# Stage one of the second batch without folds, its pairs spread wider, two weight parts loaded sooner

## The chip, the core and the metric

The kernel runs on one core of a Trainium2 chip. The metric is device time in microseconds (us) of that core. Engines are named PE (TensorE), DVE (VectorE), ACT (ScalarE), POOL (GpSimd) and SP (SyncE, which here only issues DMAs); PEld is the weight load of PE.

## The reference

Eight batches of 3008 x 256 tokens go through a Fourier layer (a real transform along the 3008 tokens, a complex 256 x 256 product with a bias, a soft threshold, the transform back), and all 24064 tokens then go through a two-layer network of width 2048 with a squared ReLU:

```python
X = np.fft.rfft(x, axis=1)
Yr = Xr @ w_r - Xi @ w_i + b_r
Yi = Xr @ w_i + Xi @ w_r + b_i
Yr = np.sign(Yr) * np.maximum(np.abs(Yr) - lam, 0.0)   # Yi likewise
y = np.fft.irfft(Yr + 1j * Yi, n=3008, axis=1)
...
h = y.reshape(24064, 256) @ w_in
g = np.maximum(h, 0.0) ** 2
out = g @ w_out
```

## The kernel before

The transform of 3008 = 64 x 47 points is done in products. **Stage one** (`Fwd`, 13 pieces q per batch) takes a piece of x of shape 120 x 2 x 256: row n2 and its mirror image lie side by side as parts 0 and 1. `add` folds them on POOL into sum and difference (tile xs), `run` multiplies the sum with the cosine matrix and the difference with the sine matrix (two fp32 products into one psf bank, line L237), ACT copies the bank to xe (one buffer), and SP stores xe to the DRAM tensor s1. **Stage two** works on pairs of frequency groups (`Pair`, 12 per batch): load ka from s1 and the matrix kb, `fwd` (L281), split into high and low fp32r parts (kxh, kxl), the 256 x 256 mix (L302), bias and threshold, and `back` (L334), whose result is stored to the DRAM tensor s3. **Stage three** (`Back`, L441 to L445) loads du from s3 and finishes the inverse transform of a piece, and `Tokens` makes of it the seven operands yt of a Strassen product on POOL (ms and yt). **The network**: six tiles of some 500 tokens per batch, eight steps (`Step`) per tile. A step has 21 products psh with w_in (L464), the recombination on DVE (mp, mu, mv, mc), ReLU, square and a cast on ACT, the low part mg on POOL, and 12 products pso with w_out.

Batch 0 has a way of its own, ahead of all that: a **ring** of seven double pieces (`Fwd32`, folds on DVE and POOL), then 24 **units** (`Unit32`) of stage two and back in plain fp32 (L381, L395, L406). Meanwhile the network's weights, which come as doubles in 16 parts (`moe_part`), are turned on DVE and ACT into fp32r pairs (`convert`: the six operations of `bits` and `join`, L151 to L164, and then `split` or `win_sums`). Parts 0 to 9 are converted beside the units, parts 10 and 11 before the network starts, and parts 12 to 15 in the network's half-steps 1, 3, 5 and 7.

From then on everything hangs on the loop over half-steps m (two per step, 96 per batch, called slots within a batch). Beside the network of batch b, a list of jobs, each with a slot at which it is due, runs stage two of batch b+1 and stage one of batch b+2. In the steady batches a pair is due every 6.1 slots and a piece of stage one every 7.0. Beside batch 0 more must be done: stage one of batch 1 (due from slot 10.2, every 1.2 slots), then its pairs (from slot 26.0, every 4.1), and stage one of batch 2 (from slot 21.6, every 5.4). Within a pair the next load is due 3.7 slots ahead of its `fwd`.

The order of instructions on each engine is fixed when the program is built, by a planner with a simulated time line; an engine then takes them strictly in that order. `issue_after` adds an edge of order on one engine. All loads of x, ka, kb and du go through `load_next`, which chains them on SP's queue in the order of the jobs:

```python
def load_next(out, in_, eng=nc.sync):
    with tc.issue_after(chain[eng].ins):
        chain[eng] = eng.dma_start(out, in_)
```

So a load that waits for its buffer holds back all loads behind it. Buffers: xt 2, xs 1, xe 1, ka 2, kb 1, du 1 in the loop. Tiles of the conversion (big, small, dw, ds) keep their memory until the last part is converted; only then is the memory of the list SIDE (xs, xt, xe and the tiles of stage two) opened.

Of the kernel before, what the change touches and what calls it, by code (L numbers as in the profile page):

```python
# [9 lines left out]
F32 = mybir.dt.float32  # L10
# [13 lines left out]
B, S, D, FF = 8, 3008, 256, 2048  # L24
# [3 lines left out]
R, J = 5, 13  # L28
M1 = R * G
# [3 lines left out]
LAM = 0.01  # L33
NP1 = N1 + 1
FRONT = {
    "a32": 1, "b32": 1, "w320": 1, "w321": 1, "big": 5, "small": 6, "ds": 1, "dw": 4, "ka": 5, "xe": 7,
    "kv": 3, "psf": 6,
}
MAIN = {
    "xs": 1, "xe": 1, "du": 1, "kv": 1, "kp": 1, "kq": 1, "ksh": 1, "ksl": 1, "kxl": 1, "kb": 1, "yr": 1,  # L40
    "ms": 1, "mp": 1, "mu": 1, "mv": 1, "mc": 3,
}
CONV = ("big", "small", "dw", "ds")
SIDE = ("xs", "xt", "xe", "ka", "kb", "kcm", "kxh", "kxl", "kp", "kq", "ke", "kv", "ksh", "ksl", "kuh", "kul", "ku")

# [11 lines left out]
def fnet_moe(ctx: ExitStack, tc, x, w_r, w_i, b_r, b_i, w_in, w_out, bm, cm, dx, a32, c32, out):  # L59
    nc = tc.nc  # L60
    pe, act, dve, pool = nc.tensor, nc.scalar, nc.vector, nc.gpsimd
# [7 lines left out]
    am32 = const.tile([M1, 2, M1], F32, name="am32")  # L69
    dx_sb = const.tile([128, 2, 4 * N2], F32R, name="dx_sb")  # L70
    bias = const.tile([128, 2, D], F32, name="bias")
# [16 lines left out]
    def T(name, shape, dt, tag=None):  # L88
        tag = tag or name
        return pools.get(tag, phase["pool"]).tile(shape, dt, name=name, tag=tag, bufs=phase["bufs"].get(tag, 2))  # L90

    def bank(shape, name="psf"):
        return phase["psum"].tile(shape, F32, name=name, tag=name, bufs=phase["bufs"].get(name, 1))

    def copy(eng, out, in_):
        if eng is act:
            return act.copy(out=out, in_=in_)  # L97
        return eng.tensor_copy(out=out, in_=in_)  # L98
# [5 lines left out]
    chain = {}  # L104
# [7 lines left out]
    b32 = T("b32", [128, D], F32)  # L112


    def load_mix_weights():
        for j, v in enumerate((b_r, b_i)):
            with tc.issue_after(ring[3].folds[1].ins):
                pool.dma_start(b32[64 * j:64 * j + 64, :], v.unsqueeze(0).broadcast_to([64, D]))
            with tc.issue_after(ring[-1].folds[1].ins):
                pool.dma_start(bias[:, j, :], v.unsqueeze(0).broadcast_to([128, D]))  # L120
        for j, w in enumerate((w_r, w_i)):
            st = T(f"w32{j}", [128, 2, D], F32)
            w32.append(st)
            nc.sync.dma_start(st, w.rearrange("(c p) d -> p c d", p=128))
        wd = T("wd", [128, 2, D], F32, tag="small")
        wn = T("wn", [128, 2, D], F32, tag="small")
        sub(dve, wd, w32[1], w32[0])
        dve.scalar_tensor_tensor(out=wn, in0=w32[0], scalar=-1.0, in1=w32[1], op0=ALU.mult, op1=ALU.subtract)
        for j, w in enumerate((wd, wn, w32[0])):
            copy(act, wx[0][:, j], w)  # L130
            sub(dve, wx[1][:, j], w, wx[0][:, j])
# [73 lines left out]
    class Fwd:  # L205
# [23 lines left out]
        def add(self):  # L229
            self.u = T("xs", [M1, 2, D], F32)  # L230
            for t in range(2):
                self.fold(pool, self.u[:, t:t + 1], t)

        def run(self):
            ps = bank([128, 2, D])
            for t in range(2):
                nc.tensor.matmul(ps[:M1, t], am32[:, t], self.u[:, t], start=True, stop=True)  # L237
            self.ev = T("xe", [M1, 1, 2, D], F32)
            copy(act, self.ev[:, 0], ps[:M1])
            self.store()  # L240
# [3 lines left out]
    def store_back(b, g, ps, eng):  # L244
        uh = T("kuh", [128, D], F32R)
        ul = T("kul", [128, D], F32R)
        done = copy(act, uh, ps)
        if eng is None:
            sub(dve, ul, ps, uh)
        else:  # L250
            u = T("ku", [128, D], F32)
            done = copy(act, u, ps)
            sub(eng, ul, u, uh)
        rows = s3[b].rearrange("m p c -> (m p) c")
        for v, m in ((uh, 4 * g), (ul, 128 + 4 * g if 4 * g < 64 else 32 + 4 * g)):
            nc.sync.dma_start(rows[m * NP:m * NP + 128], v.bitcast(F32))
        return done


    class Pair:  # L260
# [70 lines left out]
        def back(self, g):  # L331
            ps = bank([128, 512])
            for n, (j, r) in enumerate(((0, self.sh), (1, self.sh), (0, self.sl))):
                nc.tensor.matmul(  # L334
                    ps[:, :D], self.cm[:, g, j * 128:(j + 1) * 128], r[:, g], start=n == 0, stop=n == 2
                )
            store_back(self.b, self.g + g, ps[:, :D], None)

# [240 lines left out]
    def fwd_tasks(b, start, step):  # L581
        jobs = []
        for q in range(J):
            f, at = Fwd(b, q), start + q * step
            jobs += [(at - 2.5, f.load), (at - 0.8, f.add), (at + 0.3, f.run)]
        return jobs
# [17 lines left out]
    def at(items, n, *names):  # L604
        if 0 <= n < len(items):
            for name in names:
                getattr(items[n], name)()

    ring = [Fwd32(0, q, 2) for q in range((J + 1) // 2)]
    units = [Unit32(0, g) for g in range(G)]  # L610
    parts = [moe_part(q) for q in (0, 1, 8, 9, 2, 3, 10, 11, 4, 5, 12, 13, 6, 7, 14, 15)]
# [8 lines left out]
    with tc.issue_after(ring[2].last.ins):  # L620
        load_mix_weights()


    EARLY, LATE = 2, 6
    LATER = {1: 12, 3: 13, 5: 14, 7: 15}

    def convert(n, after=None):
        p = parts[n]
        p.bits(after)
        p.join()  # L630
        if n % 4 > 1:
            p.split()
        elif n % 4:
            win_sums(n // 4, parts[n - 1:n + 1])

    last = ring[-1].last
    for p in parts[:EARLY]:
        with tc.issue_after(last.ins):
            p.load()
        last = p.get  # L640
# [4 lines left out]
    for r in range(-5, len(units) + 3):  # L645
        at(units, r + 5, "load")
        at(units, r + 1, "fwd", "bins")
        at(units, r - 1, "shrink")
        at(units, r - 2, "back", "store")
        at(units, r, "mix")  # L650
        while loads and loads[0][0] <= r:
            p = loads.pop(0)[1]
            with tc.issue_after((units[r + 5] if r + 5 < len(units) else units[-1]).get.ins):
                p.load()
        for n, k in paced:
            if k + 3 == r:
                convert(n, units[k])
    with tc.issue_after(ring[-1].folds[1].ins):
        pool.dma_start(dx_sb, dx)
    chain[nc.sync], chain[pool] = units[-1].get, ring[-1].folds[1]  # L660
    front.close()
    phase.update(
        pool=memory(ctx, "main"), bufs={**{k: FRONT[k] for k in CONV}, **MAIN, "psf": 2}, psum=memory(ctx, "main_ps", space=PSUM)
    )

    pairs = [[Pair(b, j) for j in range(G // 2)] for b in range(B)]
    steps = [Step(t, n) for t in range(len(tiles)) for n in range(NF // 2)]
    slots = len(HALF) * NF
    first = sorted(back_tasks(0, 0), key=lambda j: j[0])
    for name in ("load", "mm", None):  # L670
        for _, job in first:
            if (job.__name__ if job.__name__ in ("load", "mm") else None) == name:
                job()
    for n in range(len(parts) - LATE, len(parts) - LATE + 2):
        convert(n, units[-1])
    jobs = []
    for m in range(2 * len(steps) + 4):
        b, r = divmod(m, slots)
        if r == 0 and b < B:
            jobs = [(t - slots, job) for t, job in jobs]  # L680
            if b + 1 < B:
                first, step = 1.0, 6.1
                if b == 0:
                    first, step = 26.0, 4.1
                    jobs += fwd_tasks(1, 10.2, 1.2) + [(first - 0.8, pairs[1][0].load)]
                jobs += pair_tasks(pairs[b + 1], first, step)
            if b + 2 < B:
                first, step = (2.6, 7.0) if b else (21.6, 5.4)
                jobs += fwd_tasks(b + 2, first, step) + [(95.0, pairs[b + 2][0].load)]
            for j in range(len(HALF)):  # L690
                t = b * len(HALF) + j + 1
                if t < len(tiles):
                    jobs += back_tasks(t, NF * j + 0.5)
            jobs.sort(key=lambda j: j[0])
        n, k = divmod(m, 2)
        if k and 0 <= n - 2 < len(steps):
            steps[n - 2].out(1)
        if n < len(steps):
            (steps[n].second if k else steps[n].first)()
        if not k and 0 <= n - 2 < len(steps):  # L700
            steps[n - 2].out(0)
        if m in LATER:
            convert(LATER[m], steps[n])
        if m == max(LATER):
            conv.close()
            pools.update(dict.fromkeys(CONV), **dict.fromkeys(SIDE, memory(ctx, "side")))
        while jobs and jobs[0][0] < r + 1:
            jobs.pop(0)[1]()
# [86 lines left out]
```

## Time and profile before

| what | us |
|---|---|
| median of 3 runs | 2666.55 |
| lowest, highest | 2664.07, 3630.81 |
| the profiled execution's own time | 2664.53 |
| its span, first to last instruction | 2662.8 |

The profile is of one execution. Its page gives busy times of the engines; its views give them by stretch of the span, with the TensorE clock that was granted (1.00 is full speed), or list groups of instructions, the chain of work that ended last, and the waits. A product in fp32 stands as two matmul records, one in fp32r as one.

### The profile page before, as it was taken

What the parts mean: (1) busy time and instruction counts of PE and PEld (TensorE: products, weight loads), DVE (VectorE), ACT (ScalarE), POOL (GpSimd) and SP (SyncE); (2) the same over time, 40 slices, a digit from 0 to 9 for tenths busy, and PEclk for the clock granted to TensorE, in tenths of its full rate; (3) what the DMA queues carried; (4) which work ended last, traced back from release to release, by engine and by line L of the source; (5) the groups of instructions that cost most, each with busy time, mean ns of one, the idle gap of its engine ahead of it and who ended that gap; (6) DMA issues with size and microseconds to landing.
All of it is one profiled execution on the core that took longest, in us unless ns stands there. A gap on an engine that the chain in (4) does not pass through costs nothing.

```text
span 2662.8 us, 47497 instructions
## 1 busy us (share of the span) xinstructions
PE 2578.3 (97%) x16856; PEld 2353.4 (88%) x16856; DVE 1786.7 (67%) x3797; ACT 1675.3 (63%) x2432; POOL 1678.3 (63%) x1656
## 2 busy tenths in 40 slices
PE   6788989999999999999999999999999999999999
PEld 4677978899999999999998999999999999999998
DVE  6873766576676767667676776757766667766554
ACT  3455655566666666666666666666666666666665
POOL 3266655567666666766676666766766666666564
PEclk8898989999999999999999999999999999999999
DMA  8614333333332333323333233323333222221100
GB/s 250 209 49 123 103 115 90 100 105 100 105 96 77 100 104 106 91 74 106 110 96 88 83 103 104 98 88 95 105 101 98 67 83 80 86 64 40 39 16 16
DMA packets 191262, 250.50 MB, mean 94 GB/s; under 512 B 21755, under 2 KB 135667, under 8 KB 191027
## 3 DMA queue, kind: packets, MB, share of 16 engines
q1 hardware_dynamic: 178627, 224.85, 27.2%
q0 software_dynamic: 12400, 22.61, 3.7%
q8 instruction: 135, 2.21, 0.3%
q14 instruction: 100, 0.82, 0.1%
HBM read 146.85 MB, written 100.53 MB: 93 GB/s over the span
## 4 chain that ended last, share of the span: by engine, by line
PE 90%; DVE 3%; DMA 3%; issue 1%; POOL 1%; ACT 1%; SPq 0%; POOLq 0%; ACTq 0%; DVEq 0%
PE pso L464 38%; PE psh L464 34%; PE psf L302 7%; PE psf L281 3%; PE psf L237 3%; PE psf L334 2%; PE psf L444 1%; PE psf L445 1%; PE psf L441 1%; PE psf L395 1%; POOL mg L101 1%; DMA kb<-bm_in 1%; DMA s<-xe 1%; DMA du<-s 0%; PE psf L353 0%
## 5 line engine op out<-in xcount | busy, mean ns | idle before, releaser
L101 POOL TENSOR_TENSOR mg<-mc,mg 128x500 fp32r<-128x500 f32 (+1 forms) x768 | 974.0, 1289 | 596.4 <-ACT mg L97 536.7
L464 PE MATMUL pso<-mg,wout 128*128 128x500 f32 (+1 forms) x4608 | 1179.6, 393 | 1.8 <-ACT mg L97 1.3
L464 PE MATMUL psh<-yt,win 128*128 128x250 f32 (+1 forms) x8064 | 1083.2, 282 | 14.1 <-DVE mc L464 8.2
L464 PEld LDWEIGHTS psh<-yt,win 128*128 128x128 f32 x8064 | 1029.0, 190 | 48.4 <-issue 8.9
L464 ACT ACTIVATE mc<-mc 128x1000 f32<-128x1000 f32 (+1 forms) x768 | 802.6, 1045 | 414.1 <-DVE mc L464 404.4
L464 PEld LDWEIGHTS pso<-mg,wout 128*128 128x128 f32 x4608 | 822.4, 189 | 134.2 <-POOL mg L101 3.3
L464 DVE TENSOR_TENSOR mc<-psh,mv 128x500 f32<-128x500 f32 (+3 forms) x768 | 419.3, 547 | 432.6 <-PE psh L464 400.1
L97 ACT CAST mg<-mc 128x1000 fp32r<-128x1000 f32 (+1 forms) x384 | 397.0, 1034 | 19.0 <-ACT mc L464 0.4
L464 DVE TENSOR_TENSOR mv<-psh,mu 128x500 f32<-128x500 f32 (+1 forms) x384 | 260.8, 679 | 56.1 <-PE psh L464 23.1
L302 PE MATMUL psf<-wx,kxh 128*128 128x256 f32 x1008 | 209.4, 284 | 3.9 <-ACT kxh L97 2.9
L98 DVE COPY mp<-psh 128x250 f32<-128x250 f32 (+1 forms) x384 | 159.9, 416 | 51.2 <-PE psh L464 28.6
L216 POOL TENSOR_TENSOR xs<-xt 120x256 f32<-120x256 f32 x182 | 133.2, 752 | 88.8 <-DMA xt<-x_in 82.9
L302 PEld LDWEIGHTS psf<-wx,kxh 128*128 128x128 f32 x1008 | 167.7, 190 | 8.6 <-ACT kxh L97 3.6
L101 POOL TENSOR_TENSOR ksl<-kv,ksh 128x512 fp32r<-128x512 f32 x84 | 108.6, 1293 | 105.4 <-ACT ksh L97 105.4
L464 DVE TENSOR_TENSOR mu<-psh,mp 128x250 f32<-128x250 f32 (+1 forms) x384 | 160.7, 419 | 11.7
L464 DVE TENSOR_TENSOR mc<-psh,mp 128x250 f32<-128x250 f32 (+1 forms) x384 | 157.1, 409 | 7.4 <-PE psh L464 5.6
L323 DVE TENSOR_TENSOR kv<-psf,ke 64x256 f32<-64x256 f32 x336 | 141.8, 422 | 21.7 <-PE psf L302 10.6
L302 PE MATMUL psf<-wx,kxl 128*128 128x256 f32 x504 | 142.1, 282 | 2.4 <-DVE kxl L101 2.4
L97 ACT COPY dy<-psf 128x188 f32<-128x188 f32 x256 | 76.5, 312 | 92.7 <-PE psf L445 92.4
L314 DVE TENSOR_TENSOR ke<-psf,bias 128x512 f32<-128x512 f32 x84 | 58.0, 691 | 106.5 <-PE psf L302 106.3
L97 ACT CAST kuh<-psf 128x256 fp32r<-128x256 f32 x192 | 68.2, 373 | 92.6 <-PE psf L334 71.9
L451 DVE TENSOR_TENSOR yr<-psf,dy 128x188 f32<-128x188 f32 (+4 forms) x256 | 78.0, 313 | 72.1 <-ACT dy L97 65.2
(94 smaller groups left out, 2538.3 us busy)
## 6 DMA issues: line engine op xcount, KB each, us to landing
du<-s SPq DMA_DIRECT2D x128, 256.0 KB, 2.8
s<-kuh SPq DMA_DIRECT2D x192, 128.0 KB, 1.8
s<-kul SPq DMA_DIRECT2D x192, 128.0 KB, 1.8
s<-xe SPq DMA_DIRECT2D x92, 240.0 KB, 2.4
xt<-x_in SPq DMA_DIRECT2D x91, 240.0 KB, 3.2
kcm<-cm_in POOLq DMA_DIRECT2D x84, 256.0 KB, 3.2
ka<-s SPq DMA_DIRECT2D x84, 256.0 KB, 3.2
du<-s SPq DMA_DIRECT2D x256, 64.0 KB, 2.7
```

The lines of the kernel that those rows point to most:

```text
L97: return act.copy(out=out, in_=in_)
L98: return eng.tensor_copy(out=out, in_=in_)
L101: return eng.tensor_tensor(out=out, in0=a, in1=b, op=ALU.subtract)
L216: return eng.tensor_tensor(out=out[:, :n], in0=self.xt[:, :n, 0], in1=self.xt[:, :n, 1], op=(ALU.add, ALU.subtract)[t])
L237: nc.tensor.matmul(ps[:M1, t], am32[:, t], self.u[:, t], start=True, stop=True)
L281: nc.tensor.matmul(pv[:, :, c, g, :], self.a[:, g, c * 128:(c + 1) * 128], bg, start=True, stop=True)
L302: self.last = nc.tensor.matmul(ps, l, wx[j][:, k, c, :], start=n == 0, stop=n == 5)
L314: dve.tensor_add(out=self.e, in0=self.pe, in1=bias)
L323: dve.tensor_add(out=v[64 * r:64 * r + 64, g], in0=ps[gs], in1=self.e[gs, r])
L334: nc.tensor.matmul(ps[:, :D], self.cm[:, g, j * 128:(j + 1) * 128], r[:, g], start=n == 0, stop=n == 2)
L451: dve.tensor_add(out=o, in0=ps[:, 0, lo:hi], in1=y[:, c, lo:hi])
L464: last_of[eng] = op(*args, **kwargs)
```

## The change

Stage one of batch 1 becomes a class `Fwd2`, which has no folds: each of its two results is the sum of two fp32 products, taken straight from the two parts of xt, the second of the sine result with a negated matrix (nam). Pieces 0 and 1 are run, and 0 to 2 loaded, ahead of the half-step loop; the others are due every 0.9 slots from slot 0.5. Its pairs are due from slot 11.2 every 5.5 slots, and stage one of batch 2 from slot 14.6 every 6.0.

Weight parts 0 and 1 are queued on SP behind the store of ring piece 1 rather than behind the last one. Part 12 is converted ahead of the loop, parts 13 to 15 in half-steps 1, 3 and 5. The broadcasts of the biases go from POOL's queue early on to SP's at unit round 4, and the load of dx_sb, too, is placed at that round. To find memory for xt and xe ahead of the loop, the buffers of big, small and dw fall from 5, 6 and 4 to 4, 4 and 3.

```diff
-    "a32": 1, "b32": 1, "w320": 1, "w321": 1, "big": 5, "small": 6, "ds": 1, "dw": 4, "ka": 5, "xe": 7,
+    "a32": 1, "b32": 1, "w320": 1, "w321": 1, "big": 4, "small": 4, "ds": 1, "dw": 3, "ka": 5, "xe": 7,
...
-    "ms": 1, "mp": 1, "mu": 1, "mv": 1, "mc": 3,
+    "ms": 1, "mp": 1, "mu": 1, "mv": 1, "mc": 3, "nam": 1,
...
-SIDE = ("xs", "xt", "xe", "ka", "kb", "kcm", "kxh", "kxl", "kp", "kq", "ke", "kv", "ksh", "ksl", "kuh", "kul", "ku")
+SIDE = ("xs", "ka", "kb", "kcm", "kxh", "kxl", "kp", "kq", "ke", "kv", "ksh", "ksl", "kuh", "kul", "ku")
...
-            with tc.issue_after(ring[-1].folds[1].ins):
-                pool.dma_start(bias[:, j, :], v.unsqueeze(0).broadcast_to([128, D]))
...
+    class Fwd2(Fwd):
+        def add(self):
+            pass
+
+        def run(self):
+            ps = bank([128, 2, D])
+            for t in range(2):
+                for i in range(2):
+                    nc.tensor.matmul(
+                        ps[:M1, t], nam if t and i else am32[:, t], self.xt[:, 0, i], start=i == 0, stop=i == 1
+                    )
+            self.ev = T("xe", [M1, 1, 2, D], F32)
+            copy(act, self.ev[:, 0], ps[:M1])
+            self.store()
...
-    LATER = {1: 12, 3: 13, 5: 14, 7: 15}
+    LATER = {1: 13, 3: 14, 5: 15}
...
-    last = ring[-1].last
+    last = ring[1].last
     for p in parts[:EARLY]:
         with tc.issue_after(last.ins):
             p.load()
...
+        if r == 4:
+            with tc.issue_after(units[8].get.ins):
+                for j, v in enumerate((b_r, b_i)):
+                    nc.sync.dma_start(bias[:, j, :], v.unsqueeze(0).broadcast_to([128, D]))
+                last_pool = pool.dma_start(dx_sb, dx)
...
-    with tc.issue_after(ring[-1].folds[1].ins):
-        pool.dma_start(dx_sb, dx)
-    chain[nc.sync], chain[pool] = units[-1].get, ring[-1].folds[1]
+    chain[nc.sync], chain[pool] = units[-1].get, last_pool
...
-    for n in range(len(parts) - LATE, len(parts) - LATE + 2):
+    for n in range(len(parts) - LATE, min(LATER.values())):
         convert(n, units[-1])
+    nam = T("nam", [M1, M1], F32)
+    act.mul(nam, am32[:, 1], -1.0)
+    second = [Fwd2(1, q) for q in range(J)]
+    for q in range(3):
+        second[q].load()
+        if q:
+            second[q - 1].run()
...
-                    first, step = 26.0, 4.1
-                    jobs += fwd_tasks(1, 10.2, 1.2) + [(first - 0.8, pairs[1][0].load)]
+                    first, step = 11.2, 5.5
+                    for q in range(2, J):
+                        if q > 2:
+                            jobs += [(0.9 * (q - 3), second[q].load)]
+                        jobs += [(0.5 + 0.9 * (q - 2), second[q].run)]
+                    jobs += [(first - 0.6, pairs[1][0].load)]
...
-                first, step = (2.6, 7.0) if b else (21.6, 5.4)
+                first, step = (2.6, 7.0) if b else (14.6, 6.0)
```

## Rows read from the trace of the kernel before

**Rows 1.** The page: busy time of each engine, its share and instructions.

```profile
PE 2578.3 (97%) x16856; PEld 2353.4 (88%) x16856; DVE 1786.7 (67%) x3797; ACT 1675.3 (63%) x2432; POOL 1678.3 (63%) x1656
```

**Rows 2.** Windows: length; busy and instructions of PE, PEld, DVE, ACT, POOL; clock, DMA, GB/s.

```profile
40.00:116.00 76.00, 67.33 (x332) 57.79 (x330) 71.06 (x155) 40.56 (x117) 22.85 (x22) 0.98 0.75 235
116.00:128.00 12.00, 4.25 (x16) 3.62 (x17) 8.17 (x17) 3.16 (x9) 0.00 (x0) 0.62 0.64 198
128.00:180.00 52.00, 40.38 (x218) 35.87 (x218) 48.08 (x91) 28.54 (x41) 27.46 (x24) 0.83 0.11 31
...
240.00:262.00 22.00, 14.53 (x52) 10.29 (x52) 2.77 (x8) 6.92 (x13) 13.99 (x18) 0.69 0.44 133
262.00:360.00 98.00, 97.42 (x663) 90.21 (x662) 71.83 (x147) 62.72 (x91) 58.52 (x58) 1.00 0.34 100
360.00:395.00 35.00, 27.17 (x147) 23.66 (x146) 18.18 (x42) 15.03 (x31) 22.59 (x26) 0.81 0.47 133
...
450.00:458.00 8.00, 4.77 (x33) 4.38 (x33) 6.21 (x13) 4.77 (x7) 7.45 (x7) 0.92 0.32 95
...
504.00:520.00 16.00, 11.26 (x54) 9.90 (x53) 3.79 (x8) 6.38 (x9) 10.93 (x12) 0.79 0.28 81
...
1000.00:1400.00 400.00, 399.31 (x2696) 368.62 (x2696) 278.31 (x595) 264.27 (x384) 269.32 (x269) 1.00 0.32 97
```

**Rows 3.** The chain that ended last, 177 to 185 us: start, length, what.

```profile
177.94 2.73 PE pso L464 x12
180.67 2.45 PE psh L464 x21
...
184.03 0.87 PE psf L237 x4
```

**Rows 4.** The same chain through the stall at 240 us.

```profile
241.10 2.91 DMA du<-s
...
254.36 1.04 POOL yt L101
...
255.45 1.86 PE psh L464 x7
```

**Rows 5.** Timeline of SP, 160 to 243 us: start, length, line, operation, count.

```profile
160.33 26.43 SPq L108 DMA_DIRECT2D xt<-x_in  x4
...
240.21 1.48 SPq L108 DMA_DIRECT2D du<-s  x3
```

**Rows 6.** Timeline of POOL: first and thirteenth pair of folds, fifteen in all.

```profile
178.72 1.44 POOL L216 TENSOR_TENSOR xs<-xt 120x256 f32<-120x256 f32 x2
...
245.23 1.41 POOL L216 TENSOR_TENSOR xs<-xt 120x256 f32<-120x256 f32 x2
```

**Rows 7.** Timeline of SP in the stall at 360 us.

```profile
368.94 0.33 SPq L108 DMA_DIRECT2D kb<-bm_in  x1
...
373.00 1.47 SPq L108 DMA_DIRECT2D du<-s  x3
```

**Rows 8.** The chain that ended last, 504 to 520 us.

```profile
506.56 2.37 DMA s<-xe
...
509.37 2.70 DMA kb<-bm_in
```

**Rows 9.** Groups of DVE instructions, 36 to 122 us: count, busy and mean, idle before.

```profile
L153 DVE SCALAR_TENSOR_TENSOR df<-da,df 128x512 int32<-128x512 int32 x12 | 8.8, 742 | 0.0
...
L151 DVE TENSOR_SCALAR df<-dst 128x512 int32<-128x512 int32 x12 | 4.9, 417 | 4.6 <-DMA dst<-w_in_in 4.6
L101 DVE TENSOR_TENSOR win<-ds,win 128x1024 fp32r<-128x1024 f32 x3 | 3.7, 1220 | 0.6 <-ACT win L97 0.4
```

**Rows 10.** Timeline of all engines, 28 to 37 us.

```profile
28.21 0.62 ACT L97 CAST wx<-w 128x512 fp32r<-128x512 f32 x1 [8.11 <-DMA w<-w_r_in]
...
36.92 0.43 DVE L151 TENSOR_SCALAR df<-dst 128x512 int32<-128x512 int32 x1 [4.64 <-DMA dst<-w_in_in]
```

**Rows 11.** Stores of xe, 180 to 260 us: count, ns min, median, max, first and last start.

```profile
L226 SPq DMA_DIRECT2D s<-xe x14: 316/317/492, 186.8 to 253.0; - x14
```

## The prediction

> **What bounds the kernel now.** I read the page's busy times first: PE is busy for 2578.3 of 2662.8 us, and no other engine for more than 67% [rows 1]. Then the windows, to see where PE is not fed. In the steady stretch from 1000 to 1400 us PE takes 2696 instructions in 400 us, 0.1484 us each, and is never idle [rows 2]: whatever PE is given there lengthens the run, and whatever is taken from POOL, DVE or ACT gives nothing. With that price I ask of each early stretch how long its PE instructions would have taken, and call the rest lost. That holds idle time and time at a lower clock together. From 262 to 360 us, 663 x 0.1484 = 98.4 us stand against 98: nothing is lost. The lost time lies in five places [rows 2]:
> - 128 to 180 us: 52 - 218 x 0.1484 = 19.6 us. DVE is busy for 48.1 of the 52: the first network steps and four weight conversions share it.
> - 240 to 262 us: 22 - 52 x 0.1484 = 14.3 us, at a mean clock of 0.69. The chain of waits shows why: du lands at 244, then POOL makes ms and yt between folds xs until 255.4, and only then do the psh products of the next tile begin [rows 4].
> - 360 to 395 us: 13.2 us; 450 to 458 us: 3.1 us; 504 to 520 us: 8.0 us, by the same sum.
>
> Together 58 us. Ahead of 116 us PE does other products and DVE sets the pace (71.1 of 76 us busy from 40 to 116), and from 116 to 128 the engines wait for the first du. What the change can win lies in these stretches.
>
> **The change part by part.** *Folds and products.* Thirteen pieces lose two POOL folds each (1.44 us a pair, [rows 6]) and gain two fp32 products each. A run of two products takes 0.87 us on the chain [rows 3], so 13 x 0.87 = **+11.3 us of PE work**. This is the one sure cost, since PE is the bound.
>
> The page Perfetto Trace Analysis of the Trainium skill (section Identifying the Most-Contended Engine) would judge PE's headroom by the busy share of weight loads. That is 88% here [rows 1], and 92% in the steady stretch, and by this rule the 11.3 us could hide in the rest. Counting disagrees: there the matmul records leave 0.7 us of 400 idle [rows 2]. By the rule the sum below would be 11.3 us lower; it is a rival.
>
> *The stall at 240 us.* Before, loads of xt sat on SP from 160.3 to 186.8 us [rows 5], because their pace is that of the folds: POOL starts the first pair at 178.7 and the thirteenth at 245.2, 5.5 us apart [rows 6], behind mg and with a single xs buffer. The du of the next tile stands behind them in the same chain and is issued at 240.2 [rows 5], some 15 us ahead of the first psh that needs it. After the change the last xt load is due at slot 8.1 and the next tile's du at slot 16.5, and POOL has no folds left between its ms and yt. I take **-13** (between -14.3, all of it, and -9, if a ramp of the clock remains).
>
> *128 to 180 us.* Eleven of the thirteen runs fall due in slots 0.5 to 9.5, where PE had 19.6 us that it did not use; each is 1.74 us of PE and asks nothing of DVE. Part 12's six operations leave the stretch: 41 us for twelve parts is 3.4 us each (six groups like the two in [rows 9]). Three parts stay, 3 x 3.4 us, with one `win_sums` of 4.5 us (three of them held DVE for 13.5 us; their largest step alone is 3.7, [rows 9]). PE's need for the same steps becomes 218 x 0.1484 + 11 x 1.74 = 51.5 us, DVE's 48.1 - 3.4 = 44.7: they change places as the bound. Some of the start cannot be filled, since the first steps still wait for conversions. I take **-10** of the lost time (from -14, half of the idle DVE left over, to -4, if the runs line up with the steps that PE could do anyway). What the runs cost is already in the 11.3.
>
> *Ahead of the loop.* Conversion of part 12 and the runs of pieces 0 and 1 (2 x 1.74 us, twice that at half clock) now stand ahead of the first step; DVE is idle for 3.8 of the 12 us and PE for 7.8 [rows 2], waiting for du. The covers are about as large as the work: **+2** (0 to +7, where 7 is both runs at half clock with no cover). The three xt loads come behind the first tile's du on SP, so they hold up only the second tile's, which is not needed for eight steps.
>
> *Pairs wider apart.* The stall at 360 us is of the kind at 240: a du load is issued at 373.0, behind a kb load that itself left at 368.9 [rows 7]. kb has one buffer, so its load waits for the `fwd` of the pair before. That `fwd` is due 4.1 - 3.7 = 0.4 slots ahead of the load before the change, 5.5 - 3.7 = 1.8 after, and 6.1 - 3.7 = 2.4 in the steady batches, which lose nothing. 1.8 lies seven tenths of the way from 0.4 to 2.4, so I take seven tenths of 13.2: **-9** (0 to -13.2). The 3.1 us at 450 sit in the last dense pairs: **-2.5** (0 to -3.1). At 504 us the last xe of batch 2 is stored at 506.6, and the first pair's kb lands at 512, which PE waits for [rows 8]. Its slot hardly moves (86.7 to 86.9); it was late because the chain was. **-5** (0 to -8.0).
>
> *The weight parts moved forward.* At 36.9 us DVE had waited 4.6 us for the first part [rows 10], and two conversions and a `win_sums` (2 x 3.4 + 4.5 = 11.3 us) then stand in front of the units in a stretch that DVE bounds. Loaded ahead, they fill DVE's idle time before 37 us. Against it: the mix weights, for which ACT waited 8.1 us [rows 10], now queue behind 1 MB more. The last ring store and the first unit hang on that, and 1 MB is 4.5 us at the 235 GB/s of [rows 2]. The biases and dx_sb leave that queue. **-5** (-10, nearly all of the 11.3, to +4, the delay alone). The smaller buffer counts, the biases on SP and nam I take at nothing: they are a few issues of 0.3 to 0.5 us beside a queue that waits; if that cover fails they cost 1 us.
>
> **Sum** against the profiled execution's 2664.5 us: -5 + 2 - 10 + 11.3 - 13 - 9 - 2.5 - 5 = -31.2, so **2633 us**. The median is 2 us above that execution, which is within the spread of the two lower runs; I leave it out. With the ends that belong to this course, 2617 to 2649.
>
> **The rivals.** *The stalls of the second half stay* (0.2). 5.5 and 6.0 slots are still under the steady 6.1 and 7.0, and everything hangs in the one chain on SP. Then 9, 2.5 and 5 do not come: 2633 + 16.5 = 2650. For it: the stall at 504 hardly changes its slots. Against it: the gap of 1.8.
>
> *Stage one becomes the late one, and the kernel is slower* (0.12). Each piece must go through PE, an ACT copy into the one xe buffer, and a store that stands in SP's queue with the loads. Before, 14 stores took 66.2 us, 5.1 each [rows 11]; that pace may be SP's and ACT's own and not POOL's. If run, copy (0.6 us, as for the cast of 512 columns in [rows 10]) and store (2.4 us, [rows 8]) follow each other without overlap, and each run waits half a block of network products for its turn on PE (1.3 us of the 2.5 to 2.7 in [rows 3]), a piece takes 1.74 + 0.6 + 2.4 + 1.3 = 6 us, and the thirteenth is stored at 125 + 13 x 6 = 203. Slot 11.2, where PE in its fixed order meets the first pair, lies near 186: 128, and 5.6 steps of 2.45 + 2.73 us [rows 3], and 19 us of runs, and some 10 still lost. The pair's load takes 2.7 more [rows 8], so PE waits 203 + 2.7 - 186 = 20 us; the pairs then run late and the 16.5 us above stay lost too: 2633 + 20 + 16.5 = 2670. It is slower than before from a wait of 15 us on, which is a pace of 5.6 us. Against it: with two xt buffers and two banks the parts of neighbouring pieces overlap, and the longest is 3 us, copy and store.
>
> *Everything comes* (0.08): the lower ends of all terms, -10 + 0 - 14 + 11.3 - 14.3 - 13.2 - 3.1 - 8 = -51.3, 2613.
>
> *The added products are free* (0.05): 2633 - 11.3 = 2622.
>
> **How the numbers follow.** The forecast has 0.55, the rivals the rest. The range 2613 to 2660 holds the forecast, the free products and most of the first rival, and leaves out the slower case and half of the best one. 2% of 2666.55 is 53 us, about what a measurement of this kernel can tell from no change: faster needs less than 2613, slower more than 2720. Only half of the best case passes the one, and the slower rival would have to lose 50 us more to pass the other: 0.05, 0.93, 0.02.
>
> **What would show it.** Right: the fold group of POOL down by 26, L237-like products up by 26; no PE gap with a low clock near 240 us; du issued well ahead of the tile; DVE on the first parts before 35 us; PE dense from 140 us on; the span of the steady batches unchanged. Wrong: PE waiting for kb or ka near slot 11, ACT copies of xe that wait for the store before, a gap at 360 or 500 us, or a first unit later than 43 us with units no faster.

## The result and the profile after

The changed kernel takes 2632.24 us (median of four runs, 2631.56 to 2632.64). The kernel before took 2664.07 us beside it, the median of three runs; a fourth, slow one took 3630.81 us and is left out. The ratio is 0.988, with a 95% interval from 0.986 to 0.9899. The forecast was 2633 us. The profiled execution of after takes 2632.53 us, its span is 2630.8 us (before 2662.8), so 32.0 us of span went away.

The page's line of busy times answers to [rows 1]. PE has 52 records more: 26 fp32 products of two records each. POOL has 28 fewer: the 26 folds, and the two broadcasts of the biases (the run with the biases moved alone has these two fewer as well, 1654).

```profile
PE 2569.7 (98%) x16908; PEld 2349.9 (89%) x16908; DVE 1781.6 (68%) x3797; ACT 1670.4 (63%) x2433; POOL 1654.5 (63%) x1628
```

The windows of after, with the columns and edges of [rows 2]:

```profile
40.00:116.00 76.00, 63.24 (x319) 54.52 (x317) 68.70 (x151) 38.72 (x112) 22.24 (x22) 0.97 0.74 227
116.00:128.00 12.00, 6.68 (x23) 5.56 (x24) 8.87 (x23) 3.78 (x12) 0.00 (x0) 0.50 0.69 202
128.00:180.00 52.00, 51.50 (x302) 45.35 (x302) 40.08 (x79) 31.66 (x48) 21.82 (x21) 0.99 0.46 133
...
240.00:262.00 22.00, 15.34 (x84) 13.62 (x83) 13.47 (x20) 9.02 (x15) 15.68 (x19) 0.77 0.29 82
262.00:360.00 98.00, 98.00 (x664) 90.63 (x663) 66.35 (x147) 60.96 (x91) 57.12 (x58) 1.00 0.37 107
360.00:395.00 35.00, 27.97 (x184) 25.70 (x183) 21.10 (x44) 17.09 (x29) 22.99 (x26) 0.90 0.35 104
...
450.00:458.00 8.00, 8.00 (x54) 7.33 (x54) 3.62 (x7) 3.76 (x7) 4.62 (x4) 1.00 0.49 150
...
504.00:520.00 16.00, 16.00 (x107) 14.62 (x107) 13.37 (x30) 11.25 (x18) 13.02 (x13) 1.00 0.38 114
...
1000.00:1400.00 400.00, 399.44 (x2686) 368.34 (x2685) 276.01 (x583) 262.67 (x379) 271.62 (x272) 1.00 0.33 97
```

The steady batches are unchanged. From 128 to 180 us PE is now busy 51.5 of 52 us at a clock of 0.99. 90 of its 302 records there are products of `Fwd2`, 0.2175 us each (0.87 for four, [rows 3]), the other 212 cost the prediction's 0.1484: 51.0 us of work in 52. The gaps at 450 and 504 us are gone. Those at 240 and 360 are not.

To see where the time went I priced PE's records by shape and called the rest of each stretch lost. The prices are psh 0.117 (2.45 for 21) and pso 0.2275 (2.73 for 12) from [rows 3], an fp32 product's record 0.2175, and the pairs' products 0.11 to 0.12 (1.38 for twelve on the chain below). With 0.11 for a record of stage three and 0.435 for one of 512 fp32 columns every cell holds within 0.5 us. The table also has the experiments of the next section.

| lost PE time, us | 0 to 128 | 128 to 240 | 240 to 262 | 262 to 520 | span |
|---|---|---|---|---|---|
| before | 52.6 | 21.1 | 13.1 | 30.5 | 2662.8 |
| everything ahead of the loop | 51.3 | 20.6 | 14.3 | 30.9 | 2659.7 |
| products at the old slots | 52.7 | 20.3 | -0.2 | 25.7 | 2653.0 |
| folds on POOL, early | 51.1 | 20.5 | 6.3 | 9.7 | 2632.0 |
| change with dense pairs | 50.9 | 1.1 | -0.4 | 24.6 | 2630.9 |
| after | 51.6 | 1.6 | 10.6 | 10.7 | 2630.8 |
| after, clamp in its bank | 50.5 | 1.2 | 6.0 | 11.1 | 2627.3 |
| the three together | 52.3 | 2.6 | 6.0 | 8.2 | 2627.9 |

From before to after: -1.0 - 19.5 - 2.5 - 19.8 = -42.8, and +11.3 for the products is -31.5, against 32.0 measured. So the sum closes; the other rows close to within 3 us in the same way. Its terms are not the predicted ones, though.

At 240 us the cause of [rows 4] and [rows 5] is gone: the last store of the second batch's stage one is started at 186.1 us ([rows 11]: 253.0), and the du for which the tile waited leaves SP at 224.5. These are the stores from 120 to 200 us (as in [rows 11]):

```profile
L224 SPq DMA_DIRECT2D s<-xe x13: 316/317/522, 130.8 to 186.1; - x13
```

The timeline of SP, with the du of the tile at 240 us and, as in [rows 7], kb and du in the gap that stays behind 360:

```profile
224.53 1.56 SPq L108 DMA_DIRECT2D du<-s  x3
...
371.58 0.33 SPq L108 DMA_DIRECT2D kb<-bm_in  x1
371.98 1.56 SPq L108 DMA_DIRECT2D du<-s  x3
```

Something else stands in its place. This is the chain that ended last, through the new gap:

```profile
243.30 1.38 PE psf L300 x12
...
248.28 4.39 DVE kc L323
252.68 0.02 issue
252.70 0.70 DVE kv L101
253.40 0.02 issue
253.43 0.63 ACT ksh L97
254.05 0.04 issue
254.10 0.80 PE psf L332 x2
...
375.33 2.17 DVE kc L323
```

The pairs start at slot 11.2 now instead of 26, so one of them meets the tile's end here. PE's order puts the pair's products (L332) ahead of all but the first two of the next tile's, and they wait for a chain of DVE steps in which one clamp of 128x512 takes 4.39 us; the same clamp has a median of 0.56 us. At 375 us there is another, of 2.17. Long clamps are not new: before, their longest was 2.27 us. POOL's timeline shows the neighbour:

```profile
247.21 0.71 POOL L101 TENSOR_TENSOR ms<-yr,ms 128x250 f32<-128x250 f32 x1
247.87 0.57 POOL L108 DMA_DIRECT2D kcm<-cm_in  x1
248.46 2.47 POOL L101 TENSOR_TENSOR mg<-mc,mg 128x504 fp32r<-128x504 f32 x2
250.87 0.48 POOL L471 COPY yr<-dy 128x368 f32<-128x368 f32 x1
251.32 1.06 POOL L101 TENSOR_TENSOR yt<-ms,yt 128x500 fp32r<-128x500 f32 x1
```

The clamp ends at 252.67, when POOL's last operation of that train has ended (252.38).

At the front, the first unit product starts at 34.56 us instead of 38.66, and the first du is issued at 113.75 instead of 117.83. The weights for the mix come 3.5 us sooner than in [rows 10], and DVE has the first part at 27.17 (before 36.92), by the timeline of all engines:

```profile
24.71 0.62 ACT L97 CAST wx<-w 128x512 fp32r<-128x512 f32 x1 [3.07 <-DMA w<-w_r_in]
...
27.17 0.42 DVE L149 TENSOR_SCALAR df<-dst 128x512 int32<-128x512 int32 x1
```

In the DVE groups from 20 to 122 us the wait of 4.6 us for dst [rows 9] is gone, and there is a thirteenth part:

```profile
L149 DVE TENSOR_SCALAR df<-dst 128x512 int32<-128x512 int32 x13 | 5.3, 416 | 0.0
```

### The profile page after: what moved, and what is told of

Read it like the earlier page. It is cut to its first block, busy times and chain, and to the rows that moved or that the text cites. A ratio compares the mean times of both kernels' runs of the same rounds, so it can differ in the third digit from the quotient of the medians.

```text
span 2630.8 us, 47549 instructions
## 1 busy us (share of the span) xinstructions
PE 2569.7 (98%) x16908; PEld 2349.9 (89%) x16908; DVE 1781.6 (68%) x3797; ACT 1670.4 (63%) x2433; POOL 1654.5 (63%) x1628
## 4 chain that ended last, share of the span: by engine, by line
PE 91%; DMA 3%; DVE 3%; POOL 2%; ACT 1%; issue 1%; SPq 0%; POOLq 0%; ACTq 0%; DVEq 0%
PE pso L478 38%; PE psh L478 34%; PE psf L300 7%; PE psf L279 3%; PE psf L235 2%; PE psf L332 2%; PE psf L458 1%; PE psf L459 1%; PE psf L455 1%; DMA du<-s 1%; POOL mg L101 1%; PE psf L346 1%; PE psf L409 1%; DMA x<-x_in 0%; DMA s<-xe 0%
## 5 line engine op out<-in xcount | busy, mean ns | idle before, releaser
L478 PE MATMUL psh<-yt,win 128*128 128x250 f32 (+1 forms) x8064 | 1072.4, 281 | 0.0
L478 DVE TENSOR_TENSOR mu<-psh,mp 128x250 f32<-128x250 f32 (+1 forms) x384 | 160.6, 418 | 11.7
L214 POOL TENSOR_TENSOR xs<-xt 120x256 f32<-120x256 f32 x156 | 114.6, 754 | 84.9 <-DMA xt<-x_in 76.7
L97 ACT CAST ksh<-kv 128x512 fp32r<-128x512 f32 x84 | 52.0, 619 | 114.5 <-DVE kv L101 114.3
```

The source lines that it names most:

```text
L214: return eng.tensor_tensor(out=out[:, :n], in0=self.xt[:, :n, 0], in1=self.xt[:, :n, 1], op=(ALU.add, ALU.subtract)[t])
L478: last_of[eng] = op(*args, **kwargs)
```

## The experiments

The theory was the prediction's: folds on POOL hold back the xt loads, these hold back du, and spacing the pairs clears the rest. The first rival is that the place is what counts: PE gets work from 128 us on, where it had none, whichever engine folds. The second is that the spacing decides. Each ratio below is to the kernel before, run beside that experiment. These medians of before differ by 2 us from group to group (2662.19 to 2664.36), so between kernels of different groups the ratios say more than the microseconds.

**Two parts loaded late again**, in the changed kernel.

```diff
-    last = ring[1].last
+    last = ring[-1].last
```

> The changed kernel with weight parts 0 and 1 queued behind the last ring store again, nothing else undone. Theory (the two parts fill DVE's idle time ahead of the units): the first du, issued at 113.8 us in the changed kernel, goes back to 117 to 119, and the time to 2636 to 2638. Rival (the broadcasts and dx_sb, taken out of the early queue, made the front shorter): du stays near 114 and the time within 1.5 us of 2632.

2630.61 us, ratio 0.9872 [0.9856, 0.9889]: no slower than the change. The first unit starts at 33.04 us, the first du is issued at 112.49, both about 1.4 us sooner than in the change. The front's relief does not come from these parts.

**Two parts forward alone**, in the kernel before: the reverse of that line.

> The kernel before with one line changed: weight parts 0 and 1 queued behind the store of ring piece 1. The prediction's theory (the parts fill DVE's idle time): 5 us less than before, the first du issued near 113. Second theory, after the run with the parts late kept its 114 us front: no gain, within 2 us of before, or up to 3 us slower, because 1 MB stands ahead of the mix weights and the last ring stores and the time of the units does not shrink with DVE's share.

2662.12 against 2662.19 us, ratio 0.9997 [0.9988, 1.0006]. The timeline shows both sides of the prediction's term, and the first du leaves at 118.20 us, no sooner (before 117.83): DVE starts on the first part at 33.30 us instead of 36.92, and the mix weights come at 30.84 instead of 28.21.

```profile
30.84 0.62 ACT L97 CAST wx<-w 128x512 fp32r<-128x512 f32 x1 [9.87 <-DMA w<-w_r_in]
...
33.30 0.76 DVE L151 TENSOR_SCALAR df<-dst 128x512 int32<-128x512 int32 x2
```

**Biases and dx moved, alone**, in the kernel before.

```diff
-            with tc.issue_after(ring[-1].folds[1].ins):
-                pool.dma_start(bias[:, j, :], ...)
...
+        if r == 4:
+            with tc.issue_after(units[8].get.ins):
+                for j, v in enumerate((b_r, b_i)):
+                    nc.sync.dma_start(bias[:, j, :], ...)
+                last_pool = pool.dma_start(dx_sb, dx)
```

> The kernel before with only the bias broadcasts and the load of dx_sb moved, as in the change. Second theory (these three DMAs, issued by POOL at 19.4 to 20.5 us, held back the mix weights and ring stores; the front's gain is theirs): the first ka lands 4 to 6 us sooner than 38.6 us, and the time is 4 to 6 us less than before. Rival (the front gained by the smaller ring of buffers or by chance of the planner): no change.

2660.66 us, ratio 0.9993 [0.9984, 1.0002]. The first unit comes at 35.63 us, 3.0 sooner, but du at 117.56, only 0.3 sooner: the units gave it back.

**The smaller buffer counts with that move**, in the kernel before.

```diff
-    ... "big": 5, "small": 6, "ds": 1, "dw": 4, ...
+    ... "big": 4, "small": 4, "ds": 1, "dw": 3, ...
```

> The kernel before with the smaller front buffer counts (big 4, small 4, dw 3) and the biases and dx moved as in the change; parts, conversions, folds and pairs as before. The move of the biases alone gave 2660.7 against 2662.2 and a first du at 117.6 us; the whole change has its first du at 113.8. If the counts are what brings the front forward, the first du is issued near 113.5 and the median is near 2658, 4 us under the kernel before. The rival, that the counts are only room for nam and the runs and cost nothing: first du at 117.5, median 2660 to 2661, as with the biases alone.

2659.93 against 2662.29 us, ratio 0.9987 [0.9978, 0.9996]. First unit at 34.09, du at 114.10: these are the times of the change. So the counts with the move bring the whole 4 us of the front. The median is 2.4 us lower, nearer to the rival's 2660 than to 2658, and that the front's gain is what reaches the end is not shown: the second tile's output comes 5.6 us later than before (275.25 against 269.65) and the sixth's 4.6 sooner (521.23 against 525.85), so the gain lies behind 262 us. Why fewer buffers help was not tried.

**Part 12 ahead of the loop, alone.**

```diff
-    LATER = {1: 12, 3: 13, 5: 14, 7: 15}
+    LATER = {1: 13, 3: 14, 5: 15}
...
-    for n in range(len(parts) - LATE, len(parts) - LATE + 2):
+    for n in range(len(parts) - LATE, min(LATER.values())):
```

> The kernel before with part 12 converted ahead of the loop (its slots in the loop 1, 3, 5 for the three parts that stay), nothing else. The prediction: its 3.4 us leave DVE where DVE is busy 48 of 52 us, so the lost time from 128 to 180 falls from 20 to about 17, and 0 to 3.4 us of it are given back ahead of the loop: 2659 to 2662. The rival, that what PE lacks there is not DVE but work of its own that it may do: the lost time stays at 20, and the conversion delays the first step, so same as before or up to 3 us slower.

2666.88 against 2662.29 us, ratio 1.0013 [1.0004, 1.0022]: slower. The lost time from 128 to 180 us hardly moves, from 20.2 to 19.6 us. DVE has 1.9 us less to do there (46.2 busy, [rows 2]: 48.1), and PE gets hardly more done for it (222 records, before 218). The first psh starts 1.0 us later (129.52 against 128.55). This is the window:

```profile
128.00:180.00 52.00, 40.08 (x222) 35.43 (x223) 46.22 (x87) 28.94 (x42) 28.31 (x25) 0.83 0.14 41
```

**Everything ahead of the loop, without the products and the pairs** (the four edits above together).

> Everything of the change that lies ahead of the loop, without the products and without the pairs: counts, biases and dx, the two parts loaded forward, part 12 ahead of the loop. By the prediction's terms (-5, and the 3.4 us of part 12 less the cover ahead of the loop) 2655 to 2658, first du near 113.5. If the single edits add up as measured so far (0.0 for the parts, -1.5 for the biases), 2660. What is then left to the full change, 2632, is the work of stage one and of the pairs: 23 to 28 us.

2661.16 us, ratio 0.9994 [0.9985, 1.0003]. The first du leaves at 112.50 us, 5.3 sooner, the third tile's first output still 1.1 us sooner (324.9 against 326.0), the sixth's 0.7 us later (526.5 against 525.9). What the front gains is lost again in the stalls that stay. The other 30 us of the change belong to stage one and the pairs.

**Products at the old slots**: in the kernel before, `Fwd2` takes the place of `Fwd` for the second batch, in the old schedule of stage one and of the pairs.

```diff
-            f, at = Fwd(b, q)
+            f, at = (Fwd2 if b == 1 else Fwd)(b, q)
```

> The kernel before with plain products in stage one of batch 1, at the old slots 10.2 to 24.6, pairs and front as before. Theory (the place is what counts, since folds at the early slots cost only 2 us more than products): 11.3 us of PE work are added where PE is full, and the stall at 240 us, whose du waited for the pace of the folds, loses most of its 13 to 14 us; 2660 to 2668, no change. Rival (sparing POOL is what counts): 2640 to 2650, with the gaps at 360 and 500 us smaller too.

2654.24 us, ratio 0.9971 [0.9961, 0.9981]. The windows show the prediction's mechanism at 240 us by itself: no POOL folds, the du of [rows 5] at 229.36 instead of 240.21, and no stall. From 128 to 180 us nothing changes. The network is 10 us behind here, since PE has the products to do (first tile's output at 209.20 us, before 199.25), so this run alone does not tell how much of the missing stall is the sooner du and how much the later need; the run with dense pairs does.

```profile
128.00:180.00 52.00, 40.29 (x218) 35.83 (x218) 48.24 (x92) 28.49 (x41) 26.20 (x22) 0.82 0.10 29
240.00:262.00 22.00, 22.00 (x139) 19.87 (x139) 10.65 (x24) 13.74 (x20) 15.55 (x19) 1.00 0.35 105
```

By the table, -0.8 - 13.3 - 4.8 + 11.3 + 0.1 = -7.5; the medians give -7.95, the spans -9.8. Both expectations miss: it is faster than the theory allowed and slower than the rival.

**Folds on POOL, early**: the change with `Fwd2` as the two POOL folds and two products of before, in the new slots (xs leaves the list SIDE for it, nam goes).

```diff
     class Fwd2(Fwd):
-        def add(self):
-            pass
-
         def run(self):
-            ps = bank([128, 2, D])
...
+            self.add()
+            super().run()
```

> The changed kernel with the folds back on POOL, each right ahead of its two products, at the new early slots; the 26 added products go. Theory (what helps is the place, early, where PE had time, and a clear SP chain, not the plain products): 2632 or less, down to 2621 if all 11.3 us of PE work were on the path, some 2626 if DVE bounds the first steps at 45 us. Rival (POOL is the engine that must be spared): 18.8 us of folds beside 21.8 us of other POOL work in 52 us delay mg and slow DVE, and the time is 2638 or more.

2634.65 us, ratio 0.989 [0.9875, 0.9905], 2.4 us above the change, and the intervals overlap; the theory had 2632 or less, the rival 2638 or more. So with the early place and the wide pairs the form of stage one decides little; at the old slots the products brought 8. The engines show the trade: 11.3 us less PE work, but 20.5 us of the stretch from 128 to 240 stay lost. This is what PE waited for from 128 to 262 us (in total, times, longest):

```profile
PE psf L235 <- POOL xs L214: 6.8, 4, 3.1
PE psh L468 <- DVE mc L468: 3.8, 1, 3.8
```

And its window, with POOL at 35.1 of 52 us:

```profile
128.00:180.00 52.00, 45.98 (x269) 41.07 (x270) 44.18 (x79) 31.20 (x44) 35.09 (x35) 0.92 0.41 115
```

**The old, dense pairs** in the changed kernel.

```diff
-                    first, step = 11.2, 5.5
+                    first, step = 26.0, 4.1
...
-                    jobs += [(first - 0.6, pairs[1][0].load)]
+                    jobs += [(first - 0.8, pairs[1][0].load)]
...
-                first, step = (2.6, 7.0) if b else (14.6, 6.0)
+                first, step = (2.6, 7.0) if b else (21.6, 5.4)
```

> The changed kernel with the old due times of the second half: pairs of batch 1 from slot 26.0 every 4.1, stage one of batch 2 from slot 21.6 every 5.4. Theory (a dense chain on SP makes the stalls): 13 to 17 us of the gain are lost, 2645 to 2649, with gaps of PE near 360, 450 and 500 us that wait for du or kb. Rival (the gaps come from DVE waiting beside POOL, whatever the spacing): within 4 us of 2632.

2636.24 us, ratio 0.9894 [0.988, 0.9909]: 4.0 us above the change, at the edge of the rival's range and not the theory's 13 to 17. The intervals overlap, and the profiled execution, the fastest of the four at 2632.65, is level with the change's. Spacing wins 13.9 us after 262 us and gives back 11.0 at 240. There, with dense pairs, PE never stops, although the network is ahead here (second tile's output at 250.75 us, before 269.65):

```profile
240.00:262.00 22.00, 22.00 (x146) 20.15 (x145) 14.45 (x32) 14.70 (x22) 11.00 (x11) 1.00 0.31 95
340.00:380.00 40.00, 33.56 (x200) 29.37 (x200) 24.10 (x53) 20.53 (x37) 25.70 (x30) 0.87 0.42 123
460.00:500.00 40.00, 33.25 (x199) 29.91 (x198) 16.58 (x39) 20.76 (x32) 23.25 (x24) 0.87 0.29 85
```

It is not that no pair runs there. A pair's products stand at the change of tiles here too (the third tile's first psh at 244.26 us). But POOL has made ms and yt of that tile by 221.6 us, its du having left at 199.1 to 201.6, and the pair's clamp takes 0.48 us, by the timelines of DVE and PE:

```profile
231.08 0.48 DVE L323 TENSOR_SCALAR kc<-kv 128x512 f32<-128x512 f32 x1
...
245.64 0.40 PE L332 MATMUL psf<-ksh,kcm 128*128 128x256 f32 x2
```

**The clamp written to the emptied bank**, in the changed kernel: kc goes to the PSUM bank that kv was read from, which is free by then.

```diff
-            ps = bank([128, 512])[:, :D]
+            bk = bank([128, 512])
+            ps = bk[:, :D]
...
-            cl = T("kc", [128, 2, D], F32, tag="ke")
+            cl = bk.rearrange("p (g d) -> p g d", g=2)
```

> The changed kernel with the clamp of the soft threshold (kc) written to the psf bank that it has just emptied, in place of SBUF, so that neither it nor the subtraction behind it has two SBUF streams. Theory (in the changed kernel kc took 4.38 us at 248 and 2.25 us at 375 because DVE waits for POOL's back-to-back work on SBUF): kc never takes over 1 us, the PE gaps near 250 and 375 us shrink, and the time is 2612 to 2624. Rival (those gaps are the planner's order, kc only the place where the wait shows): the gaps stay, within 3 us of 2632, or longer because the bank is held for 1 us more.

2630.35 us, ratio 0.9873 [0.9858, 0.9888]. The clamp (min/median/max ns) no longer waits, here first in after, then in this kernel:

```profile
L323 DVE TENSOR_SCALAR kc<-kv x84: 416/560/4382, 206.7 to 2306.2; 128x512 f32<-128x512 f32 x84
```

```profile
L324 DVE TENSOR_SCALAR psf<-kv x84: 681/684/697, 205.6 to 2301.1; 128x512 f32<-128x512 f32 x84
```

The gap at 240 shrinks by 4.6 us, the time by 1.9, with overlapping intervals; the theory's 2612 to 2624 does not come. That the long clamps hang on where the output lies is shown by the maximum, and that POOL held them by the same place: POOL runs the same train there (mg, yr, yt from 246.54 to 250.47 us), and the clamp that starts beside it at 247.44 takes 0.69 us. That the wait was worth more than 2 us of the 10.6 is not shown.

**The three together**: the change with the parts late, the clamp in its bank, and stage one of the third batch at (12.2, 6.2).

> The changed kernel with the parts late again, the clamp in the psf bank, and stage one of batch 2 due from slot 12.2 every 6.2 slots. The first two were worth 1.6 and 1.9 us by themselves: if they add, 2629; with the gap near 365 us, in which the xt load of batch 2 waits, eased by the wider slots, 2622 to 2626. Rival (the planner's order moves the gaps about and none goes): 2629 to 2634.

2628.32 us, ratio 0.9871 [0.9857, 0.9886]: 3.9 us below the change, which looks like the sum of the two (1.6 and 1.9). But the kernel before ran 2 us faster beside it, and the ratio is that of either alone (0.9872, 0.9873). So it is not shown that the two gains add, and the new slots add nothing that shows.

**The sum folded on DVE**, in that kernel: three products a piece instead of four, the fold due 0.4 slots ahead of them.

```diff
+        def add(self):
+            self.u = T("x0", [M1, 1, D], F32)
+            self.fold(dve, self.u, 0)
...
+            nc.tensor.matmul(ps[:M1, 0], am32[:, 0], self.u[:, 0], start=True, stop=True)
-            for t in range(2):
+            for t in range(1, 2):
```

> The combined kernel (parts late, clamp in the psf bank, wider stage one of the third batch; 2628.3 us) with the sum of each piece of the second batch folded on DVE (one tensor_tensor of 256 columns, about 0.41 us) into a tile of its own, so a piece takes three fp32 products instead of four: 13 x 0.435 = 5.7 us less PE work, 13 x 0.41 = 5.3 us more on DVE. If PE is bound from 128 to 240 us since the products came there, and DVE has room (it is busy 40 of 52 us from 128 to 180 in the changed kernel), the median falls to about 2623. The rival: DVE's queue is in order, a fold there waits for its xt load and holds the network's steps behind it, as the folds on POOL did; then 2628 or slower.

2627.57 us, ratio 0.9867 [0.9853, 0.988]: 0.75 below, not 5.7. The lost time from 128 to 240 rises from 2.6 to 10.0 us. In the groups of DVE from 128 to 180, ten folds take 4.7 us and keep DVE waiting for their loads for 6.7, with the network's steps behind them:

```profile
L214 DVE TENSOR_TENSOR x<-xt 120x256 f32<-120x256 f32 x10 | 4.7, 468 | 6.7 <-DMA xt<-x_in 6.7
```

## Why the prediction came true

The total was right within 1 us, and that is luck in part: two terms erred by about 10 us in opposite ways. Two of the prediction's own signs of being wrong or right failed as well: a gap with a low clock stays at 240 us (0.77), and one at 360.

- *Products, +11.3*: right. A piece's eight records take 1.73 us on the chain of after, against 1.74. Nothing of it is free in a stretch that PE fills.

```profile
172.20 1.73 PE psf L346 x8
```

- *128 to 180, -10*: mis-sized, at 19.0 by shape (20.2 lost before, 1.2 after) and 19.5 up to 240; past its own end of -14. The cause was misread with it. I called DVE the bound because it was busy 48.1 of 52 us, and took half of what it left idle as lost to PE. DVE does pace the network's steps there: the chain that ended last runs over DVE from 143.7 to 176.9 us (below). But 1.9 us less on DVE gave PE nothing, and the products, which do not hang on those steps, filled PE while DVE still did its work. PE lacked work whose inputs were there. Nor was it only the folds that kept stage one late: SP's first xt load waited for a conversion operation on DVE until 160.3 us, and with the products at the old slots until 160.6. These are SP's waits in the kernel before from 140 to 262 us (in total, times, longest):

```profile
SPq L108 <- DVE dw L160: 20.3, 1, 20.3
```

  And this is where that chain comes onto DVE and leaves it:

```profile
143.72 0.39 DVE mp L98
...
176.45 0.42 DVE mc L464
...
177.00 0.93 PE psh L464 x6
```

  The first tile paid 5.6 us for it: from the first psh to its output 70.7 us before, 76.3 after, with some 23 us more work in it.
- *Stall at 240, -13*: the mechanism was right. The stall goes with the products at the old slots (13.3), and with dense pairs (13.5), where the network is not behind. One reading was off by two products: the next tile's first two psh started at 253.53 us, not at 255.4. In the change only 2.5 came, because the third edit, pairs from slot 11.2 on, put a pair's chain, which PE waits for, beside POOL's work for the next tile; with dense pairs a pair stands there too and costs nothing. I costed the edits one by one, and did not ask what the pairs would meet where they now run.
- *Pairs and the stalls at 360, 450 and 504, -16.5*: 19.8 came after 262 us, but as net of the spacing at most 4.0 us, because it costs 11.0 at 240. The run with folds early shows 20.8. What both share is the wide pairs, which the early place makes possible; with dense pairs the early place brings 5.9 there. The reading by the gap in slots between `fwd` and load is not confirmed: at 360 us a loss of some 8 us stays, and the chain in it is DVE's, not kb's.
- *Front, -5*: the size was near (du 4.1 us sooner), the reason wrong. The parts forward bring 0.0; the counts and the biases, which I had at nothing, bring it. The two kernels with the sooner front alone are 2.4 and 1.1 us below before, the second within its interval of no change.
- *Ahead of the loop, +2*: not borne out. From du's issue to the first psh it takes 10.7 us before (117.83 to 128.55) and 12.7 after (113.75 to 126.41), which looks like the term. But the run with the counts and the biases, which has neither part 12 nor the runs ahead of the loop, takes 12.3 and has its first psh at 126.39, as late as the change; the run with part 12 alone takes 10.3. So the longer wait comes with the sooner du, and what the work ahead of the loop costs does not show there. Part 12 alone made the kernel 0.1% slower all the same.

Of the rivals, the stalls that stay (2650) came in part: one of the three stayed, with another cause. The late stage one (2670) did not come. The stores of 13 pieces lie 55.3 us apart from first to last, 4.6 each, under the 5.6 from which it decides. The free products (2622) did not come: the 51.0 us counted above fill the 52. Had the products hidden behind other work, the lost time there would come out well below nothing; it is 1.2. By the Trainium skill (Perfetto Trace Analysis, section Identifying the Most-Contended Engine) weight loads, one of the page's two measures of headroom, at 87% of that stretch, 45.35 of 52 us, would leave PE room for more; the trace does not agree.

Two figures of the prediction stand on nothing shown: it does not say which ends of its terms make 2617 to 2649, and its 2% as what a measurement can tell is far too wide, since the interval of the ratio is 0.2% to either side.

What stays open: why smaller counts bring the first unit forward, and what of the gap at 246 to 258 us is left once the clamp does not wait (6.0 us in that window, 3.7 of them waits in five places for other steps of the pair, at a mean clock of 0.92). Folds early with dense pairs were not run.

## What to carry to other kernels

When an in-order engine idles early because its inputs come late, look for independent work that can be moved there: here the place was worth 18 to 20 us (from the products at the old slots to the change with dense pairs, by the medians and by the ratios, the front's 1 to 2 included), the form 2 to 8. Cost edits together at each place where one of them puts new work: the spacing that won 14 us later took 11 us from the gap that another edit had cleared. A busy engine may pace one stream of work and still not bind the idle engine beside it; relieve it alone, or give the idle one other work, before a term is built on it.

## What the runs showed of the hardware

A DVE clamp of 128x512 from SBUF to SBUF, 0.42 us at best, took 4.38 us beside POOL. It began at 248.28 us, while POOL issued a DMA (247.87 to 248.44); four POOL operations that began after it, two mg, yr and yt, ran to their ends first. With its output in PSUM the clamp took 0.68 to 0.70 us in all 84 cases: slower at best, but never held, not even beside the same train of POOL (0.69 us at 247.44). The Trainium skill (SBUF — State Buffer, section Who interferes with whom) says that VectorE in a two-port mode and GpSimd exclude each other for a whole instruction, and that the one that issues first has it. The trace agrees on the exclusion, though no row says in which mode the clamp ran. On the order it goes further: the clamp was not let in between POOL's operations either, though it had begun before them (POOL's starts are rough in the records).
